# Five loads and stores in another order on SyncE's queue, in an attention and mixture-of-experts kernel

## The chip, the cores and the metric

The kernel runs on one core of one Trainium2 chip. The metric is the device time of one execution in microseconds (us), here the median of three runs. Engines are named as in the profile: PE (TensorE matmuls), PEld (its weight loads), DVE (VectorE), ACT (ScalarE), POOL (GpSimd) and SP (SyncE). SP does no arithmetic; it issues the plain DMA transfers, one after the other.

## The reference

The kernel computes an attention layer whose output goes through a mixture of experts. Cut to its core:

```
scores = q @ k^T / 8; kept: the first 4 keys and the last 128 up to the row's own
a = softmax(scores);  x = a @ v                  # q, k, v: 4 batches, 8 heads, 768 rows, 64 wide
x = x with a row's heads side by side            # 3072 rows of 512
logits = x @ w_gate + log1p(exp(x @ w_noise)) * noise      # 8 experts
top2 = the two best experts of each row, weights by softmax over the two
out[row] = sum over its two experts e of weight * (relu(x[row] @ w1[e]) @ w2[e])   # 512 -> 1024 -> 512
```

## The kernel before

There are two phases. Phase one, about the first 150 us, is the attention, the routing of rows to experts and the preparation of the first expert. Phase two is the experts' matmuls.

In phase one the work is cut into 16 groups, numbered 0 to 15: a batch and a pair of heads each. Every group has three units of 256 query rows, so there are units 0 to 47. A group needs two loads: its keys and queries (`load_kq`, L387, tile `kq`, three buffers) and its values (`load_v`, L390, tile `vn`, two buffers). Of a unit, PE computes the scores (L413), ACT and DVE mask and exponentiate them, PE turns the result (L502), and PE multiplies by the values (L528) and by differences of neighbouring blocks of values (L531). Those differences, tile `dv`, are made on POOL from `vn` by the helper at L320.

Results of a batch leave in two ways into one DRAM buffer, `x_rows`. The attention rows are stored by `rows_d` (L562), four DMAs for 256 rows, once DVE has transposed them (L557). When the batch is routed, the experts' weights of each row are stored beside them by `keep` (L887), four DMAs whose runs are 64 bytes long (6x16 floats a partition); they are called the weight rows below, and their source, tile `rt_w`, is finished on POOL at L883. One more DMA (L1499) fills the first 128 rows of `x_rows` with zeros from tile `zt`, for slots of an expert that hold no row.

The rows of the first expert are fetched from `x_rows` by an indirect DMA on POOL (`gather`, L1028, tile `xg`); the first three such gathers come after batch 1 is routed. The program holds the first of them until the list of its rows (`idg`, DVE L980), the attention rows and weight rows of batches 0 and 1 and the zeros have all been written. The rows are then scaled on DVE (L1080, L1082).

The experts' weights come through tile `st` (`w_chunk`, load at L1138, two buffers); ACT makes the high half (L1142) and POOL or DVE the low half (L320).

The order of all these steps in phase one is a table of numbers, `ORDER`, replayed by `Plan.replay`; every engine executes its own steps in that order. A load takes two numbers, the issue on SP and the transfer; the second emits nothing. A second table, `GATES`, holds some loads back: `803:31` keeps the load of values with number 803 behind the scores of unit 31, `1012:38` the keys of group 15 behind those of unit 38, and `856:42` the next load of values behind those of unit 42. SP waits in order, so whatever stands behind a waiting DMA waits too. The order of phase two comes from `Plan.run`, a planner with costs.

Of the kernel before, what the change touches and what calls it, by code (L numbers as in the profile page):

```python
# [80 lines left out]
"""  # L81
SIDE = """
00000101100011100111100110100100100010101001000001100110100000110001100101100000010010000010010001100000010110010000
# [1540 lines left out]
```

## Time and profile before

| | |
|---|---|
| median of 3 runs | 718.93 us (717.76 to 720.94) |
| the profiled execution | 717.77 us, of which the span of instructions is 716.1 us |
| PE busy | 703.1 us, 98% of the span |
| DVE, ACT, POOL busy | 420.1, 308.1, 386.0 us |
| DMA rate over the span | 145 GB/s |

A share over the whole span mixes the two phases. In phase two PE is the only engine that is always busy. In the stretch that the change touches, about 97 to 118 us, PE, DVE and ACT are all busy nearly all the time, and so are the DMA engines. Whether a transfer that lands earlier or later changes anything is read from the rows of that stretch: who waits for it, and how long before its use it has landed.

### The profile page before, as it was taken

Reading aid. Unit: us, or ns where it says so; the run is one execution under the profiler, and the core shown is the slowest. Engines: PE = TensorE matmul, PEld = TensorE weight load, DVE = VectorE, ACT = ScalarE, POOL = GpSimd, SP = SyncE. Lnnn points to the kernel's source line nnn. Section 1 sums busy time; section 2 is a strip of 40 time slices with the busy share of each in tenths; the row PEclk is TensorE's granted clock in tenths of the full one; section 3 lists DMA queues with packets and bytes.
Section 4 is the critical chain, followed back from the end, with each engine's and each line's share of the span. In section 5 each row is a group of like instructions: output and inputs, shape, how many; then the busy total and the mean of one; then the engine's idle time right before and its main releaser. Section 6 shows DMA issues by size and latency. Waiting matters only on the chain.

```text
span 716.1 us, 16960 instructions
## 1 busy us (share of the span) xinstructions
PE 703.1 (98%) x6580; PEld 626.3 (87%) x6580; DVE 420.1 (59%) x1008; ACT 308.1 (43%) x823; POOL 386.0 (54%) x602
## 2 busy tenths in 40 slices
PE   8999999999999999999999999999999999999996
PEld 4878787768899989989999999999999999999994
DVE  7889999988547545553564366436544734473310
ACT  6999999942244233313331343134313421442210
POOL 3647668711466755465556645663567373737012
PEclk9999999999999999999999999999999999999999
DMA  7566777777866616372737364736554560634023
GB/s 231 194 231 193 184 217 225 167 225 204 293 116 196 169 35 166 129 189 52 178 129 174 62 170 145 167 64 177 178 109 92 165 151 26 155 119 78 6 40 45
DMA packets 68467, 104.63 MB, mean 146 GB/s; under 512 B 20112, under 2 KB 41360, under 8 KB 68384
## 3 DMA queue, kind: packets, MB, share of 16 engines
q1 hardware_dynamic: 55104, 75.71, 34.3%
q0 software_dynamic: 13280, 27.81, 20.5%
q8 instruction: 52, 0.85, 0.5%
q14 instruction: 31, 0.25, 0.1%
HBM read 72.79 MB, written 30.70 MB: 145 GB/s over the span
## 4 chain that ended last, share of the span: by engine, by line
PE 86%; DVE 4%; issue 4%; POOL 2%; DMA 2%; ACT 1%; POOLq 0%; DVEq 0%; ACTq 0%
PE H L1182 12%; PE H L1184 12%; PE H L1183 12%; PE Y L1242 8%; PE Y L1241 8%; PE Y L1240 8%; PE Y L1250 4%; PE Y L1251 4%; PE Y L1249 4%; PE D L413 4%; PE D L502 3%; PE X L528 2%; PE X L531 2%; PE X L543 1%; POOL out L1283 1%
## 5 line engine op out<-in xcount | busy, mean ns | idle before, releaser
L1034 POOL DMA_INDIRECT xg<-x_rows,rt_idq x173 | 174.5, 1009 | 62.8 <-issue 46.1
L1182 PE MATMUL H<-skn,w 128*128 128x384 f32 (+4 forms) x508 | 174.0, 343 | 0.0
L1184 PE MATMUL H<-skn,w 128*128 128x384 f32 (+4 forms) x508 | 173.7, 342 | 0.0
L1183 PE MATMUL H<-sqn,w 128*128 128x384 f32 (+4 forms) x508 | 173.2, 341 | 0.0
L1226 ACT ACTIVATE h<-H 128x384 fp32r<-128x384 f32 (+4 forms) x127 | 63.4, 499 | 250.5 <-PE H L1184 244.8
L1231 DVE SCALAR_TENSOR_TENSOR h<-H,h 128x384 fp32r<-128x384 f32 (+4 forms) x127 | 71.5, 563 | 159.8 <-ACT h L1226 159.7
L1283 POOL DMA_INDIRECT out<-y,idx x46 | 80.8, 1756 | 52.2 <-ACT y L1278 41.0
L1183 PEld LDWEIGHTS H<-sqn,w 128*128 128x128 f32 x508 | 95.5, 188 | 5.1 <-DVE sqn L320 0.2
L1182 PEld LDWEIGHTS H<-skn,w 128*128 128x128 f32 x508 | 95.4, 188 | 5.2 <-DVE lt L753 0.3
L1292 POOL COPY spacer<-h 1x1 f32<-1x1 f32 x88 | 25.0, 284 | 133.7 <-ACT h L1226 133.4
L1184 PEld LDWEIGHTS H<-skn,w 128*128 128x128 f32 x508 | 95.3, 188 | 1.8
L457 ACT ACTIVATE cbuf<-cbuf,nb 128x132 f32<-128x132 f32 x192 | 75.1, 402 | 1.8 <-POOL nb L446 0.9
L1104 ACT ACTIVATE skn<-xtn 128x512 fp32r<-128x512 f32 (+2 forms) x46 | 27.6, 605 | 63.8 <-DVE xtn L1095 63.8
L1242 PE MATMUL Y<-w2a,h 128*128 128x512 f32 x136 | 53.9, 396 | 0.0
L1240 PE MATMUL Y<-w2a,h 128*128 128x512 f32 x136 | 53.6, 394 | 0.0
L1241 PE MATMUL Y<-w2a,h 128*128 128x512 f32 x136 | 53.5, 394 | 0.0
L1240 PE MATMUL Y<-w2b,h 128*128 128x512 f32 x136 | 53.5, 393 | 0.0
L1241 PE MATMUL Y<-w2b,h 128*128 128x512 f32 x136 | 53.4, 393 | 0.0
L1242 PE MATMUL Y<-w2b,h 128*128 128x512 f32 x136 | 53.3, 392 | 0.0
L320 DVE TENSOR_TENSOR w<-st,w 128x1024 fp32r<-128x1024 f32 x30 | 36.6, 1222 | 9.1 <-ACT w L1142 9.0
L413 PE MATMUL D<-kq 64*64 64x200 f32 (+3 forms) x832 | 39.4, 319 | 2.1 <-DVE mn L443 2.1
L320 DVE TENSOR_TENSOR sqn<-xtn,skn 128x512 fp32r<-128x512 f32 (+2 forms) x46 | 30.0, 658 | 17.0 <-ACT skn L1104 16.8
(214 smaller groups left out, 1332.3 us busy)
## 6 DMA issues: line engine op xcount, KB each, us to landing
st<-in_w1l SPq DMA_DIRECT2D x32, 512.0 KB
st<-in_w2l SPq DMA_DIRECT2D x32, 512.0 KB
kq<-in_kq SPq DMA_DIRECT2D x15, 816.0 KB
vn<-in_v SPq DMA_DIRECT2D x16, 384.0 KB
x_rows<-xr SPq DMA_DIRECT2D x48, 128.0 KB
out<-zt SPq DMA_DIRECT2D x24, 256.0 KB
y<-y_rows SPq DMA_DIRECT2D x14, 256.0 KB
xg<-x_rows,rt_idq POOLq DMA_INDIRECT x173, 2.8
```

Of the source, the lines that this page charges most:

```text
L320: eng.tensor_tensor(out, a, b, op=OP.subtract)
L413: last = nc.tensor.matmul(x[:, o:o + w], kq(g)[r, 1, j, t], k[:, f:f + w], start=True, stop=True)
L457: nc.scalar.activation(C(n)[:, u], C(n)[:, u], AF.Exp, bias=get("nb", n)[:, u:u + 1], scale=1.0 / math.sqrt(D), accum_out=get("sm", n // 2 ...
L1034: nc.gpsimd.indirect_dma_start(out=x[:, i, :], out_offset=None, in_=xbuf.rearrange("r (q d) -> (r q) d", d=sh.SW), in_offset=bass.Indirect ...
L1182: nc.tensor.matmul(p, w[:, 0], xh, start=(i == 0), stop=False)
L1183: nc.tensor.matmul(p, w[:, 0], xl, start=False, stop=False)
L1184: nc.tensor.matmul(p, w[:, 1], xh, start=False, stop=(i == sh.DM // 128 - 1))
L1231: nc.vector.scalar_tensor_tensor(h[:, width:2 * width], p, 0.0, h[:, :width].bitcast(F32), op0=OP.max, op1=OP.subtract)
L1240: nc.tensor.matmul(p, hh, w[:, 0], start=(f == 0), stop=False)
L1241: nc.tensor.matmul(p, hh, w[:, 1], start=False, stop=False)
L1242: nc.tensor.matmul(p, hl, w[:, 0], start=False, stop=(f == FC - 1))
L1283: d = nc.gpsimd.indirect_dma_start(out=out, out_offset=bass.IndirectOffsetOnAxis(ap=x[:size(e, t), t:t + 1], axis=0), in_=get("y", Y[e, t] ...
```

## The change

The numbers of five steps stand at other places in `ORDER`. 1132 is the load of the first quarter of `w2` of the first expert. 803 is the load of the values of group 12. 948 and 1012 are the loads of the keys of groups 14 and 15. The weight rows of batch 1 (696) and the zeros (1116) keep their own places and change sides with the loads that move. No instruction is added or removed, and no engine's work but SP's is in another order.

```
@@ ORDER, two of its lines @@
-646 693 734 809 676 666 679 699 700 820 701 698 704 702 648 643 793 810 718 754 692 821 382 694 680 420 755 735 811 513
+1133 686 646 693 734 809 676 666 679 699 700 820 701 698 704 702 648 643 793 810 718 754 692 821 382 694 680 420 755 735
-607 814 1131 756 860 803 804 741 846 766 696 697 742 705 757 707 683 815 743 708 861 758 767 796 862 893 710 746 744 769
+814 1131 756 860 741 846 766 696 697 803 804 948 949 1012 1013 742 705 757 707 683 815 743 708 861 758 767 796 862 893
```

On SP, from the stores of batch 1's attention rows to the values of group 13, this stood before (`x4`: four DMAs in a row):

```order
L562 DMA x_rows<-xr 32x8x128 x8
L1138 DMA st<-in_w2l 128x1024
L390 DMA vn<-in_v 128x768
L887 DMA x_rows<-rt_w 128x6x16 x4
L1499 DMA x_rows<-zt 128x576
L387 DMA kq<-in_kq 128x1632 x2
L390 DMA vn<-in_v 128x768
L379 DMA vr<-in_vs 16x1024 x2
```

The load of weights stood behind both stores of attention rows, the weight rows behind the values of group 12, and both loads of keys behind the zeros. On SP this stands there now:

```order
L562 DMA x_rows<-xr 32x8x128 x4
L1138 DMA st<-in_w2l 128x1024
L562 DMA x_rows<-xr 32x8x128 x4
L887 DMA x_rows<-rt_w 128x6x16 x4
L390 DMA vn<-in_v 128x768
L387 DMA kq<-in_kq 128x1632 x2
L1499 DMA x_rows<-zt 128x576
L390 DMA vn<-in_v 128x768
L379 DMA vr<-in_vs 16x1024 x2
```

The load of weights has moved ahead of the second store of attention rows, the weight rows ahead of the values of group 12, and the keys of groups 14 and 15 to right behind those values; the zeros come last of these.

On POOL the same instructions stand in the same order; only the semaphores that they wait for have other numbers. From the differences for group 12 to the first gather, with the waits as they are now:

```order
L320 TENSOR_TENSOR dv<-vn 128x640 [waits DMAHW7_49,PE_49]
L470 TENSOR_SCALAR sm<-sm 128x8 [waits Activation_49]
L446 TENSOR_SCALAR nb<-mn 128x4 [waits Pool_49]
L1028 DMA xg<-x_rows,idg 128x576 [waits DMAHW3_49,DMAHW4_49,DMAHW2_49,DMAHW5_49,DMAHW1_49,DMAHW6_49,DMAHW0_49,DVE_49]
L446 TENSOR_SCALAR nb<-mn 128x4 [waits Pool_49]
L518 AFFINE_SELECT CM<-CT 128x256 [waits Activation_49]
```

The names `DMAHW0` to `DMAHW7` are eight semaphores that SP's DMAs use in turn. The differences still wait for the load of their values, and the gather for its writes and for DVE's list; what is behind the gather on POOL is what was behind it before.

## Rows read from the trace of the kernel before

**Rows 1.** The page's first part: busy time, share of the span, instructions of each engine.

```profile
PE 703.1 (98%) x6580; PEld 626.3 (87%) x6580; DVE 420.1 (59%) x1008; ACT 308.1 (43%) x823; POOL 386.0 (54%) x602
```

**Rows 2.** PE's waits, 95 to 150 us: who, for what, us, times, longest.

```profile
PE D L1090 <- DVE xg L1082: 0.6, 1, 0.6
...
PE X L528 <- DVE xtn L418: 0.3, 1, 0.3
```

**Rows 3.** Windows: length; PE, PEld, DVE, ACT, POOL busy; clock; DMA share, GB/s.

```profile
100.00:103.00 3.00, 3.00 (x104) 2.58 (x104) 2.81 (x12) 2.98 (x14) 2.57 (x12) 1.00 0.70 175
103.00:109.00 6.00, 6.00 (x176) 4.99 (x168) 5.79 (x17) 5.85 (x26) 3.77 (x5) 1.00 0.92 234
109.00:112.00 3.00, 3.00 (x64) 2.09 (x57) 3.00 (x7) 3.00 (x10) 2.01 (x5) 1.00 0.86 161
112.00:115.00 3.00, 3.00 (x72) 2.02 (x66) 3.00 (x9) 2.84 (x13) 3.00 (x6) 1.00 0.95 349
115.00:118.00 3.00, 2.89 (x86) 2.08 (x86) 2.72 (x9) 3.00 (x15) 2.56 (x6) 1.00 0.53 201
135.00:150.00 15.00, 13.10 (x325) 10.64 (x324) 13.36 (x33) 10.56 (x41) 9.02 (x17) 1.00 0.60 142
```

**Rows 4.** Timeline of SP: start, us until the last is issued, line, transfer.

```profile
97.97 2.23 SPq L562 DMA_DIRECT2D x_rows<-xr  x4
...
101.38 2.25 SPq L562 DMA_DIRECT2D x_rows<-xr  x4
103.73 0.41 SPq L1138 DMA_DIRECT2D st<-in_w2l  x1
105.98 0.36 SPq L390 DMA_DIRECT2D vn<-in_v  x1
106.43 3.27 SPq L887 DMA_DIRECT2D x_rows<-rt_w  x4
109.75 0.53 SPq L1499 DMA_DIRECT2D x_rows<-zt  x1
110.33 2.61 SPq L387 DMA_DIRECT2D kq<-in_kq  x2
117.78 0.33 SPq L390 DMA_DIRECT2D vn<-in_v  x1
...
134.52 0.42 SPq L390 DMA_DIRECT2D vn<-in_v  x1
```

**Rows 5.** Timeline of POOL; in brackets the idle time before and its releaser.

```profile
102.35 0.22 POOL L883 COPY rt_w<-rt_w 128x48 f32<-128x48 f32 x1
...
113.88 1.54 POOL L320 TENSOR_TENSOR dv<-vn 128x640 f32<-128x640 f32 x1
...
116.28 1.23 POOL L1028 DMA_INDIRECT xg<-x_rows,idg  x1 [0.23 <-issue]
...
117.75 1.00 POOL L518 TENSOR_SCALAR_AFFINE_SELECT CM<-CT 128x256 f32<-128x256 f32 x2
...
138.57 1.55 POOL L320 TENSOR_TENSOR dv<-vn 128x640 f32<-128x640 f32 x1
```

**Rows 6.** Timeline of DVE: transposes, list of the gather, first use of gathered rows.

```profile
100.59 0.76 DVE L557 STREAM_TRANSPOSE xr<-xtn 128x256 f32<-128x256 f32 x2
...
115.83 0.15 DVE L980 SCALAR_TENSOR_TENSOR idg<-D,ga 128x3 int32<-128x3 f32 x1
...
120.17 0.22 DVE L1080 TENSOR_SCALAR xg<-xg 128x16 f32<-128x16 f32 x1
```

**Rows 7.** Timeline of PE: scores (L413) and multiplications by the values.

```profile
105.25 0.66 PE L528 MATMUL X<-CT,vn 128*64 128x128 f32 x8
...
116.89 1.49 PE L413 MATMUL D<-kq 64*64 64x132 f32 x36
...
119.16 0.39 PE L531 MATMUL X<-CM,dv 128*64 128x128 f32 x4
```

**Rows 8.** Timeline of ACT: the high half of the moved load of weights.

```profile
109.61 1.05 ACT L1142 ACTIVATE w2a<-st 128x1024 fp32r<-128x1024 f32 x1
```

30 rows, old and new, of the table ORDER are left out of this document.

## The prediction

> **What bounds the kernel now.** I read the busy shares first: PE works 703.1 of 716.1 us, so at most 13.0 us of the span are not matmul time [rows 1]. Next the waits of PE in the stretch that holds the moved transfers and what follows up to the end of phase one: there are four, 1.9 us in all, the longest 0.6 us, and every one ends with DVE, ACT or POOL, none with a DMA [rows 2]. The windows say where: from 100 to 115 us PE is never idle, from 115 to 118 us it is idle for 0.11 us, and the rest of the idle time, 15.00 - 13.10 = 1.90 us, lies behind 135 us [rows 3]. DVE and ACT are nearly full in the same windows (5.79 and 5.85 of 6 us from 103 to 109), and the DMA engines are busy to 0.86 to 0.95 between 103 and 115 us. So three engines and the DMA are all close to full, but what PE waits for is computed data. A transfer that lands earlier can gain only where somebody waits for it; one that lands later costs only once its reserve is used up.
>
> **The change, transfer by transfer.** Nothing is added or removed, so the only terms are times of issue. I go along SP's queue.
>
> The load of weights now follows the first of the two stores, whose issue ends at 97.97 + 2.23 = 100.20. SP then stands idle before the second one, since its transposes run to 100.59 + 0.76 = 101.35 and its first DMA is issued at 101.38 [rows 4, 6]. An issue of 0.41 us fits into that pause: the load goes out near 100.3 instead of 103.73, some 3.4 us earlier, and the store still starts at 101.38 and ends at 103.63. The user of the load is ACT at 109.61, which comes in its order behind other work, with no idle time in brackets before it [rows 8]. Value 0.
>
> The weight rows come next. POOL has them ready at 102.35 + 0.22 = 102.57, before SP is free, so they are not held: they start at 103.7 instead of 106.43, 2.7 us earlier, and end by 103.7 + 3.27 = 107.0 [rows 4, 5]. Only the first gather needs them. It also needs DVE's list, which is ready at 115.83 + 0.15 = 115.98, and it starts 0.30 us after that [rows 5, 6]. DVE sets it, so the gain is 0.
>
> The values of group 12 fall back. Before they were issued at 105.98, right behind the multiplication that frees their buffer (105.25 + 0.66 = 105.91) [rows 4, 7]. Now they go out at about 107.0, 1.0 us later. How long such a load takes is bounded by the last group's: issued at 134.52, used by POOL at 138.57, so it lands within 4.05 us [rows 4, 5]. That gives 111.1 at the latest here, and POOL takes them at 113.88: 2.8 us of reserve. Value 0.
>
> The keys of groups 14 and 15 go out at about 107.4 to 110.0 instead of 110.33 to 112.94. Their gate, the scores of unit 38, stands on PE ahead of the multiplication that starts at 105.25, so it holds nothing [rows 7]. PE uses the first of them at 116.89, with no idle time in brackets, so landing sooner gains 0 [rows 7].
>
> The zeros change from 109.75 to about 110.0 at the issue, 0.25 us, but two loads of keys are now ahead of them. This is the one edit that can cost, because the first gather waits for the zeros too. I take the DMA engines' work from the windows: 0.70x3 + 0.92x6 + 0.86x3 + 0.95x3 + 0.53x3 = 14.64 us between 100 and 118 [rows 3]. The changed kernel has the load of weights ready in the slack of the first window, so that I let the engines run at 0.92 throughout: 14.64 / 0.92 = 15.9, and the last of it, the zeros among it, is through at 115.9. That is just as the list is ready (115.98). The bounds are 114.6 (engines full from 100 on) and 118.0 (nothing won). At 114.6 the gather is not held at all; at 118.0 it is held for 2.0 us. Value 0, by the middle case.
>
> From 117.78 on SP's queue is as before: the next load of values is held there by unit 42's scores, which started at 116.89 [rows 4, 7]. So nothing of the new order is carried past this point by SP.
>
> The sum is 0.0 us against the profiled execution's own 717.77 us. That execution stands 1.16 us below the median of the three runs, 718.93; I forecast for the median 718.8 us.
>
> **A rule that speaks against the new order.** The window with most of the weight rows moves 161 GB/s at a DMA share of 0.86, the next one, with the keys, 349 GB/s at 0.95 [rows 3]. The Trainium skill, "DMA: Bandwidth & Descriptors", Specifications, gives 512 bytes as the least transfer for full rate; these runs have 64 bytes. The trace agrees that the engines are occupied with few bytes there. By that rule the weight rows, put ahead, would push the values back by their whole stretch.
>
> **The rivals.** *Slower, by the zeros.* The DMA engines take what SP issues in turn, so the zeros land with the last of the keys, later than 116.4. The Trainium skill, "DMA: Bandwidth & Descriptors", Queues, rings and completion order, says that each DMA engine takes the descriptors of one queue in ring order; no row here shows which packet went first. The gather stands on POOL ahead of the selections (117.75) that PE needs at 119.16 [rows 5, 7]. The first is done by half of 1.00 us, 118.25, the second by 118.75, so PE has 0.4 us of reserve; a gather held for 2.0 us costs 2.0 - 0.4 = 1.6 us. For it speaks that POOL has no way around a held gather; against it the estimate of 115.9. Time: 718.93 + 1.6 = 720.5.
>
> *Slower, by the weight rows.* If they hold the DMA engines for as long as one window, 3.0 us, the values land at 111.1 + 3.0 = 114.1 and POOL is held for 0.2 us at 113.88; against it stands the 4.05 us, which is an upper bound. Time: at most 719.1.
>
> *Faster.* The keys are through before the gathers' rows are fetched, so the gathers find free DMA engines, and DVE's chain runs ahead. For it: the DMA share is 0.53 from 115 to 118 us and could be lower. Against it: DVE takes the first gathered rows at 120.17 with no idle time in brackets, so it did not wait for them [rows 6]. The most that can be won is the idle time of PE behind 135 us, 1.9 us, if all of it went: 717.0.
>
> *The change does nothing*, since the weight rows are not ready and hold the values: POOL's 102.57 against 103.7 on SP speaks against it, and the time would be that of before or of the second rival.
>
> **How the numbers follow.** No change: 0.70, with 717.3 to 720.0 as its own range (the sum at the profiled execution and at the median, with the runs' scatter around it). Slower by the zeros: 0.17, 718.9 to 720.5. Faster: 0.10, 717.0 to 718.9. The weight rows or no effect: 0.03. A measurement of this kernel can tell about 0.5% from no change, 3.6 us. No case reaches this bound: the dearest is 1.6 us and the best gain 1.9 us. What is left for over 3.6 us is a median that drifts, since the three runs lie 3.2 us apart, together with a wait behind 118 us that the rows of before can't show: 0.04 faster, 0.03 slower, 0.93 within. The range has to hold the two outer cases and part of that scatter: 716.6 to 720.9.
>
> **What would show it.** In the profile of the changed kernel SP should issue the load of weights at about 100.3, the weight rows from 103.7, the values near 107.0, the keys near 107.4 and the zeros near 110. The differences on POOL should start near 113.9 and the first gather near 116.3. PE's scores near 116.9 should have no idle time before them, and PE's idle time from 95 to 150 us should stay near 2 us. The first rival shows as idle time of POOL before the gather that ends with a DMA, and a wait of PE behind it for the selections. I am wrong on the whole if the idle time of PE in this stretch changes by more than 2 us, or if phase two, whose order is untouched, takes another time.

## The result and the profile after

The changed kernel takes 722.78 us (median of 11 runs, 720.80 to 725.91) against 719.55 us for the kernel before beside it on the same chip (11 runs, 717.72 to 721.06). The ratio is 1.0052 [1.0033, 1.0070]: slower by half a per cent, 3.2 us. The forecast was 718.8 us and no change that can be measured, with 0.03 for slower. It was wrong. The likeliest way to be slower had been named, the zeros that land behind the keys, but its price was set at half of what it is.

The profiled execution of the changed kernel took 723.43 us, its span is 721.8 us. The page's first part shows that the matmul time is nearly what it was [rows 1]; PE's idle time went from 13.0 to 17.3 us.

```profile
PE 704.5 (98%) x6580; PEld 626.5 (87%) x6580; DVE 420.9 (58%) x1008; ACT 308.7 (43%) x823; POOL 386.2 (54%) x602
```

The windows say where. First the kernel before from 95 to 127 us (length; busy time of PE, PEld, DVE, ACT, POOL; clock; DMA share and GB/s):

```profile
95.00:127.00 32.00, 31.84 (x817) 24.66 (x809) 30.71 (x98) 30.69 (x123) 25.11 (x54) 1.00 0.79 220
```

The same view of the changed kernel:

```profile
95.00:127.00 32.00, 28.57 (x713) 21.59 (x706) 26.91 (x82) 27.31 (x109) 22.34 (x48) 1.00 0.70 196
...
150.00:225.00 75.00, 74.18 (x477) 62.68 (x474) 48.33 (x135) 25.66 (x44) 27.84 (x43) 1.00 0.72 212
225.00:235.00 10.00, 8.63 (x55) 7.88 (x55) 7.11 (x18) 3.32 (x5) 6.88 (x9) 1.00 0.52 178
```

PE is busy 3.27 us less in the stretch of the moved transfers. The other visible gap, 1.4 us from 225 to 235 us, lies in phase two, whose order is untouched; from 150 to 240 us PE is idle for 2.19 us here, but also for 1.71 and 2.11 us in two of the kernels below that take the time of before (weight rows alone, zeros early), so I count it as scatter. The same windows in steps of 3 us, of the changed kernel:

```profile
103.00:106.00 3.00, 3.00 (x64) 2.42 (x66) 2.99 (x9) 3.00 (x13) 2.24 (x3) 1.00 0.94 252
106.00:109.00 3.00, 3.00 (x104) 2.61 (x107) 2.80 (x8) 2.83 (x13) 1.33 (x4) 1.00 0.56 61
109.00:112.00 3.00, 3.00 (x52) 2.00 (x44) 3.00 (x7) 3.00 (x10) 2.23 (x7) 1.00 0.91 294
112.00:115.00 3.00, 2.89 (x67) 1.94 (x64) 3.00 (x8) 2.83 (x13) 3.00 (x5) 1.00 0.96 348
115.00:118.00 3.00, 2.17 (x50) 1.03 (x50) 2.14 (x8) 2.01 (x10) 0.56 (x3) 1.00 0.39 150
118.00:121.00 3.00, 2.45 (x48) 1.74 (x46) 2.14 (x7) 2.54 (x11) 1.43 (x3) 1.00 0.38 97
```

From 115 us on all four compute engines have idle time, POOL by far the most (0.56 of 3.00 us against 2.56 before, [rows 3]). Before that the DMA engines run at 0.56 of their time and 61 GB/s from 106 to 109 us, where the kernel before has a share of 0.92 over 103 to 109 us [rows 3]: the DMA work did not come forward as the forecast assumed. SP's timeline shows why (columns as in [rows 4]):

```profile
100.00 0.41 SPq L1138 DMA_DIRECT2D st<-in_w2l  x1
101.04 2.71 SPq L562 DMA_DIRECT2D x_rows<-xr  x4
103.85 3.98 SPq L887 DMA_DIRECT2D x_rows<-rt_w  x4
107.93 0.49 SPq L390 DMA_DIRECT2D vn<-in_v  x1
108.46 0.91 SPq L387 DMA_DIRECT2D kq<-in_kq  x2
109.42 0.43 SPq L1499 DMA_DIRECT2D x_rows<-zt  x1
```

Until 107.93 only weight rows are issued, 3.98 us long and few bytes. Then values, both loads of keys and the zeros go out within 1.9 us. The zeros are issued 0.33 us earlier than before (109.75, [rows 4]), with 2 x 816 KB of keys just ahead.

When the zeros land is seen on POOL's sequencer, whose waits the profile lists under POOLq. Ahead of the first gather it waits for one semaphore after another; the row gives the number of these waits, the shortest, median and longest in ns, and when the first and the last began. The kernel before:

```profile
L1028 POOLq EVENT_SEMAPHORE  x3: 43/43/300, 113.7 to 113.8; - x3
```

The changed kernel:

```profile
L1028 POOLq EVENT_SEMAPHORE  x4: 17/43/5020, 113.3 to 118.5; - x4
```

Before, the longest wait is 0.30 us and the last begins at 113.8, so all the writes have landed by about 114.1. Now one wait lasts 5.02 us, and the last one begins at 118.5. The semaphore events of the trace say what the long wait is for: the semaphore of one store of weight rows, complete at 108.92, and that of the zeros. A DMA from SP adds sixteen completions to its semaphore, and the sixteenth of the zeros comes at 118.38 us, 9.0 us after the issue (before at 114.11, 4.4 us after it). Fifteen of them are in by 116.88; the last one alone is 1.5 us later. POOL then, in the changed kernel:

```profile
113.55 1.54 POOL L320 TENSOR_TENSOR dv<-vn 128x640 f32<-128x640 f32 x1
...
115.50 0.23 POOL L446 TENSOR_SCALAR nb<-mn 128x4 f32<-128x4 f32 x1
119.52 1.23 POOL L1028 DMA_INDIRECT xg<-x_rows,idg  x1 [3.80 <-PE D L413]
120.79 0.24 POOL L446 TENSOR_SCALAR nb<-mn 128x4 f32<-128x4 f32 x1
120.98 1.00 POOL L518 TENSOR_SCALAR_AFFINE_SELECT CM<-CT 128x256 f32<-128x256 f32 x2
```

The differences start at 113.55, no later than before (113.88, [rows 5]), so the values were in time. The gather stands 3.80 us later than POOL could start it; before it was 0.23 us [rows 5]. The name in the bracket, a score of PE, is a coincidence of ends: the instruction order of the changed kernel gives the gather seven waits for DMA and one for DVE, none for PE, and the experiments below show other names there. Between the last of the waits (118.5) and the start of the gather lies 1.0 us. DVE is next. Its list is ready at 115.49 + 0.16 = 115.65, and it has 2.50 us of idle time until the gathered rows land:

```profile
115.49 0.16 DVE L980 SCALAR_TENSOR_TENSOR idg<-D,ga 128x3 int32<-128x3 f32 x1
...
121.11 0.35 DVE L821 SCALAR_TENSOR_TENSOR rt_ab<-lg 128x48 f32<-128x48 f32 x1
123.97 0.28 DVE L1080 TENSOR_SCALAR xg<-xg 128x16 f32<-128x16 f32 x1 [2.50 <-DMA xg<-x_rows,idg]
124.28 0.69 DVE L1082 TENSOR_TENSOR xg<-xg 128x512 f32<-128x512 f32 x1
124.89 0.45 DVE L436 COPY_PREDICATED cbuf<-le,D 128x256 f32<-128x256 uint8 x1
```

Before, the first use of the gathered rows stands at 120.17 without a wait [rows 6]. And PE, its rows with idle time in this stretch:

```profile
117.44 0.63 PE L742 MATMUL D<-xtn,wbd 128*32 128x256 f32 x4 [0.83 <-issue]
118.00 1.49 PE L413 MATMUL D<-kq 64*64 64x132 f32 x36
...
121.45 0.44 PE L531 MATMUL X<-CM,dv 128*64 128x128 f32 x4 [1.00 <-POOL CM L518]
...
125.40 0.81 PE L413 MATMUL D<-kq 64*64 64x132 f32 x20 [1.43 <-DVE cbuf L436]
```

Three gaps, 0.83 + 1.00 + 1.43 = 3.26 us, are nearly all of the 32.00 - 28.57 = 3.43 us that PE is idle in the window; the kernel before has 0.16 us there. Two of them follow from the gather: PE waits for the selections that stand behind it on POOL, and then for a copy (L436) that stands on DVE behind the use of the gathered rows. The first gap, inside one step's matmuls, has no releaser; it comes while the gather is held, but the profile doesn't tie it to the gather. PE's other waits up to 150 us are three of the four of [rows 2]; the fourth now lies behind 150 us.

### The profile page after: what moved, and what is told of

It is laid out like the page before. It is cut to its first block, busy times and chain, and to the rows that moved or that the text cites. A ratio compares the mean times of both kernels' runs of the same rounds, so it can differ in the third digit from the quotient of the medians.

```text
span 721.8 us, 16961 instructions
## 1 busy us (share of the span) xinstructions
PE 704.5 (98%) x6580; PEld 626.5 (87%) x6580; DVE 420.9 (58%) x1008; ACT 308.7 (43%) x823; POOL 386.2 (54%) x602
## 4 chain that ended last, share of the span: by engine, by line
PE 83%; DMA 5%; issue 4%; DVE 3%; POOL 2%; ACT 1%; SPq 0%; POOLq 0%; DVEq 0%; ACTq 0%
PE H L1182 12%; PE H L1184 12%; PE H L1183 12%; PE Y L1242 8%; PE Y L1241 8%; PE Y L1240 8%; PE Y L1249 3%; PE Y L1250 3%; PE Y L1251 3%; PE D L413 3%; PE D L502 3%; PE X L528 2%; PE X L531 2%; DMA kq<-in_kq 2%; PE X L543 1%
## 5 line engine op out<-in xcount | busy, mean ns | idle before, releaser
L413 PE MATMUL D<-kq 64*64 64x200 f32 (+3 forms) x832 | 39.2, 317 | 3.2 <-DVE cbuf L436 1.4
```

## The experiments

The theory: two loads of keys ahead of the zeros delay the landing of the zeros, and the first gather holds POOL, then DVE and PE. The rivals: the small transfers of the weight rows, or the load of weights, now ahead of other transfers, take DMA time where it hurts; or the early keys disturb the stretch as such, whatever the zeros do. Ratios are to the kernel before on the same chip.

**One part at a time.** Three kernels are the kernel before with one part of the change each. In the table the change moves four loads, not five steps (1132, 803, 948 and 1012); the two loads of keys move together here.

```
@@ ORDER of before: e1_weights @@
-515 516 686 646 ... 859 738 1132 1133 844
+515 516 1132 1133 686 646 ... 859 738 844
@@ ORDER of before: e2_weight_rows @@
-756 860 803 804 741 846 766 696 697 742
+756 860 741 846 766 696 697 803 804 742
@@ ORDER of before: e3_keys @@
-1134 824 1116 1117 ... 711 948 949 784 ... 785 1012 1013 1136
+1134 824 948 949 1012 1013 1116 1117 ... 711 784 ... 785 1136
```

> The kernel before with one edit: the load of weights ahead of the second store of attention rows. Theory 1 (the zeros land behind the two loads of keys and hold the first gather on POOL): zeros and keys stay in their old order, so 719.6 us like before, within 1 us; gather near 116.3. Theory 2 (the loads of keys, closer behind each other and earlier, delay PE's instruction fetch): keys stay where they were, also 719.6. Theory 3 (the load of weights crowds the stores and what follows): part or all of the 3.2 us, 721 to 723.

> The kernel before with one edit: the weight rows ahead of the values of group 12. Theory 1 and theory 2: 719.6 us, within 1 us, since zeros and keys keep their order. The rival of the prediction (the weight rows hold the DMA engines and the values come late): the differences on POOL start later than 114.5 and the time is 720.5 or more.

> The kernel before with one edit: both loads of keys ahead of the zeros. Theory 1: the zeros land after the keys, near 118.5, the gather starts near 119.5 and the time is 722 to 724 us, as long as the whole change. Theory 2: the keys are only 0.6 us earlier than before, so PE's fetch is as before, and the time is 719.6 to 720.2.

Measured: the load of weights alone 720.58 us against 721.46, 0.9993 [0.9980, 1.0005]; the weight rows alone 721.28 us, 0.9998 [0.9981, 1.0014]; the keys alone 725.45 us, 1.0052 [1.0033, 1.0071]. The first two parts cost nothing that can be measured; the third by itself has the whole ratio. The rows of the third, POOL's waits and gather:

```profile
L1028 POOLq EVENT_SEMAPHORE  x4: 17/43/7002, 113.6 to 120.8; - x4
```

```profile
121.81 1.23 POOL L1028 DMA_INDIRECT xg<-x_rows,idg  x1 [5.77 <-issue]
```

Here the zeros are issued last of all, at 113.12, have landed by 120.8, and the gather starts 1.0 us later. That is 2.3 us later than I expected, since SP takes 2.55 us to issue the two loads of keys here (0.91 us in the changed kernel). The gather is held longer than in the changed kernel, so that the two ratios are equal is partly chance. PE in the same kernel:

```profile
118.65 0.66 PE L528 MATMUL X<-CT,vn 128*64 128x128 f32 x8
123.75 0.69 PE L531 MATMUL X<-CM,dv 128*64 128x128 f32 x4 [4.44 <-POOL CM L518]
124.23 1.07 PE L528 MATMUL X<-CT,vn 128*64 128x128 f32 x8
```

The wait for the selections, 1.00 us in the changed kernel, is 4.44 us here. The eight multiplications of L528 take 0.66 us ahead of it and 1.07 us behind it: the granted clock falls, as the windows say:

```profile
121.00:124.00 3.00, 0.25 (x2) 0.25 (x4) 0.00 (x0) 0.64 (x3) 2.14 (x4) 0.87 0.16 33
124.00:127.00 3.00, 3.00 (x64) 2.67 (x66) 1.45 (x4) 1.16 (x7) 2.64 (x5) 0.56 0.47 126
```

**The zeros back in front.** If the keys disturb the stretch as such, the changed kernel stays slow when only the zeros move. Two kernels put the zeros ahead of both loads of keys and between them:

```
@@ ORDER of the changed kernel: e4_zeros_before_keys @@
-803 804 948 949 1012 1013 742 ... 824 1116 1117 759
+803 804 1116 1117 948 949 1012 1013 742 ... 824 759
@@ ORDER of the changed kernel: e8_zeros_between @@
-803 804 948 949 1012 1013 742 ... 824 1116 1117 759
+803 804 948 949 1116 1117 1012 1013 742 ... 824 759
```

> The changed kernel with the zeros put ahead of the two loads of keys. Theory 1: the zeros land before 115, the gather starts near 116 and the time is back at 719.6 us, within 1 us. Theory 2: the gather is back, but PE still has an idle gap of about 0.8 us inside the logits' matmuls (L742) near 116.6, and the time is 720.4 to 721.5.

> The changed kernel with the zeros between the two loads of keys. Theory 1 with transfers taken in turn: the zeros land behind one load of keys, 2 to 3 us earlier than in the changed kernel, near 115.5 to 116.5, so that the gather starts within 1 us of the list; ratio 0.999 to 1.002. If the zeros' landing depends on all traffic and not on the place in the queue, the gather stays near 119.5 and the ratio near 1.005.

Measured: ahead of both 720.46 us against 721.46, 0.9981 [0.9966, 0.9996]; between them 720.55 us against 721.34, 1.0004 [0.9984, 1.0024]. The loss is gone in both, with all four moved loads where the change put them, so the rivals fall. PE's gap of 0.83 us inside L742 is in neither profile. SP's issues in the second:

```profile
108.43 0.43 SPq L387 DMA_DIRECT2D kq<-in_kq  x1
108.91 0.43 SPq L1499 DMA_DIRECT2D x_rows<-zt  x1
109.38 0.43 SPq L387 DMA_DIRECT2D kq<-in_kq  x1
```

and its waits on POOL:

```profile
L1028 POOLq EVENT_SEMAPHORE  x4: 17/43/845, 113.8 to 114.8; - x4
```

```profile
116.38 1.23 POOL L1028 DMA_INDIRECT xg<-x_rows,idg  x1 [0.22 <-issue]
```

With one load of keys ahead and one behind, the zeros land at 114.72, 5.8 us after their issue, though the second keys are issued only 0.47 us after them. With none ahead they land at 114.12, 4.1 us after their issue at 110.07; with both ahead, in the changed kernel, 9.0 us after it. So transfers from SP land in the order of issue here, and 816 KB ahead cost about 2 us the first time and 3 us the second. The Trainium skill, "DMA: Bandwidth & Descriptors", Queues, rings and completion order, says that each DMA engine consumes the descriptors of a ring in order. These three landings agree.

**The zeros much earlier.** The zeros need no data of this stretch, and their gate can be an earlier unit. In the changed kernel and in the kernel before they go out far ahead of it:

```
@@ ORDER and GATES: e5_zeros_early (changed), e6_before_zeros_early (before) @@
-728 611 854 855 ... 824 1116 1117 759
+728 611 1116 1117 854 855 ... 824 759
-1116:39
+1116:33
```

> The changed kernel with the zeros put far ahead, behind the weight rows of batch 0 (with their gate set to unit 33 for that). Theory 1 (the zeros behind the keys hold the first gather, and POOL, DVE and PE wait in its wake): the gather is set by DVE's list again, and the ratio to the kernel before is 0.997 to 1.001. Theory 2 (PE's instruction fetch is late behind the closely packed keys): an idle gap of about 0.8 us inside the logits' matmuls (L742) stays, ratio 1.001 to 1.002. If the other moves of the change cost anything by themselves, the ratio stays above 1.002.

> The kernel before with the zeros put far ahead, at the same place as in the run before this one. Theory 1: in the kernel before the zeros have landed at 114.1, ahead of the list at 116.0, so nothing waits for them and the ratio is 0.998 to 1.001. If the zeros also cost the kernel before something by crowding the keys, 0.995 to 0.998.

Measured: 720.92 us, 0.9996 [0.9979, 1.0012], and 720.95 us, 0.9998 [0.9982, 1.0015], both against 721.34. Without the zeros in the queue the early keys neither cost nor gain anything that can be measured, and in the kernel before the zeros are at no disadvantage where they are.

**The gather out of the way.** If POOL's order passes the delay on to PE, the gather can be put behind the selections of the changed kernel; in a second kernel DVE's first use of the gathered rows also moves, behind five steps of DVE's:

```
@@ ORDER of the changed kernel: e9_gather_later @@
-791 865 997 839 ... 954 829 856
+791 865 839 ... 954 829 997 856
@@ ORDER of e9: e10_gather_and_use_later @@
-998 881 898 ... 852 1019 999
+881 898 ... 852 1019 998 999
```

> The changed kernel with the first gather moved on POOL behind the small step and the two selections that stood behind it; SP's order is that of the changed kernel. Theory 1: the gather still starts near 119.5, DVE still waits for the gathered rows, but PE no longer waits for the selections (1.0 us in the changed kernel); ratio 1.002 to 1.005, about 1 us below the changed kernel. If the held POOL queue is the whole cost, the ratio is back at 1.000 to 1.001; if it is only DVE's wait for the rows, it stays at 1.005.

> The changed kernel with the first gather behind the selections on POOL, as in the last run, and in addition the first scaling of gathered rows (L1080, L1082) moved on DVE behind the five steps that stood behind it; SP's order is that of the changed kernel, so the zeros are as late as there. Theory 1, taken further: the price of the late zeros is what stands behind them in POOL's and DVE's queues, and the fall of PE's clock that follows PE's idle time. Then PE's wait for DVE near 123 us (1.4 us in the run before) shrinks to under 0.5 us, the granted clock stays at 1.00, and the ratio is 0.999 to 1.002. If PE's clock falls because of the late transfers themselves, or something else in the change costs time, the ratio stays at 1.004 to 1.006.

Measured: 724.39 us against 721.34, 1.0050 [1.0033, 1.0067], and 726.39 us against 720.80, 1.0071 [1.0047, 1.0094]. Neither gives the loss back; I had expected the first about 1 us below the changed kernel, and its ratio is the same (1.0050 against 1.0052). In the first, PE's wait for the selections is gone, but DVE has 2.56 us of idle time before the first use, and PE waits 1.4 us for DVE; PE's waits from 118 to 132 us:

```profile
PE D L413 <- DVE cbuf L436: 1.4, 1, 1.4
PE D L502 <- issue: 0.4, 1, 0.4
```

That is less waiting than in the changed kernel. Its windows show what took its place:

```profile
121.00:124.00 3.00, 1.16 (x39) 0.91 (x39) 1.29 (x3) 2.35 (x10) 2.57 (x6) 1.00 0.68 191
124.00:127.00 3.00, 2.98 (x31) 2.18 (x32) 2.51 (x6) 0.40 (x2) 2.98 (x5) 0.50 0.34 98
127.00:130.00 3.00, 3.00 (x49) 2.55 (x49) 2.05 (x9) 2.56 (x11) 0.81 (x4) 0.50 0.74 178
130.00:133.00 3.00, 3.00 (x78) 2.14 (x78) 1.85 (x14) 1.94 (x8) 0.32 (x2) 0.87 0.69 177
```

The clock is 0.50, the 1.2 GHz level, for over 6 us, and PE gets 31 and 49 matmuls done in windows where the kernel before, at 1.00, has 71 and 92. Over all runs, 10 of 11 of this kernel have a mean clock of at most 0.994, of the kernel before beside it 2 of 34. So the edit shows that the chain runs through POOL's order, but the clock takes back what the shorter wait gave, and the time says little on the price of the wait. In the second, DVE:

```profile
124.25 0.23 DVE L1080 TENSOR_SCALAR xg<-xg 128x16 f32<-128x16 f32 x1
124.51 2.73 DVE L1082 TENSOR_TENSOR xg<-xg 128x512 f32<-128x512 f32 x1
```

The multiplication that takes 0.69 us elsewhere takes 2.73 us here, and PE, whose next matmuls need it, stands for 3.25 us. All 12 runs have a mean clock of 0.993 to 0.996. My expectation failed: I had taken the wait away and counted neither on the long instruction nor on the clock.

**The two versions again**, on one chip with one set of runs of the kernel before: the changed kernel with the zeros ahead of the keys, and the changed kernel as it is.

> The run with the zeros ahead of both keys once more, since its ratio was 0.9981 with an interval that ends below 1. If the rest of the change (the earlier load of weights, the weight rows ahead of the values) gains something by itself, the ratio is again 0.997 to 0.999; if that was scatter, 0.999 to 1.001.

> The changed kernel itself once more, beside the two runs above on the same chip. All theories: a ratio of 1.003 to 1.007. Theory 1 with the clock: the runs whose mean granted clock is at or under 0.994 are the longer ones, by 2 to 3 us.

Measured: 720.14 us against 720.80, 0.9982 [0.9962, 1.0003], and 723.44 us, 1.0028 [1.0003, 1.0053], just under the range that I expected. The better version stands at 0.998 both times, once clear of 1 and once not. That it beats the kernel before is not shown: with the same four loads moved and the zeros between the keys or far ahead, the ratios are 1.0004 and 0.9996. Against the changed kernel it is 720.14 / 723.44 = 0.995. The second profile of the changed kernel repeats the chain, with the zeros issued 1.75 us later:

```profile
L1028 POOLq EVENT_SEMAPHORE  x4: 17/43/4642, 115.0 to 119.8; - x4
```

```profile
120.80 1.23 POOL L1028 DMA_INDIRECT xg<-x_rows,idg  x1 [3.41 <-DVE lt L753]
```

```profile
PE X L531 <- POOL CM L518: 2.1, 1, 2.1
...
PE D L413 <- DVE cbuf L436: 0.4, 1, 0.4
```

Again 1.0 us lies between the last wait and the gather; the bracket names another releaser. PE waits 2.1 us for the selections and 0.4 us for DVE, and the gap of 0.83 us inside L742 isn't there. In the three executions whose mean clock is 0.995 or less, the time is 724.37, 725.75 and 727.76 us, above the median in each. In the first set of runs of the changed kernel the three at 0.992 to 0.994 took 725.91, 725.74 and 722.01 us, the last below the median: part of the runs' spread is the clock's, and not all of it.

## Why the prediction was wrong

- The times of issue held to about 1 us. Forecast and measured: load of weights 100.3 and 100.00, weight rows 103.7 and 103.85, values 107.0 and 107.93, keys 107.4 and 108.46, zeros 110.0 and 109.42, differences on POOL 113.9 and 113.55. The weight rows took 3.98 us where I put 3.27, which made values and keys 1 us later than forecast.
- The terms of the load of weights, the weight rows and the values, each put at 0, held: 0.9993 and 0.9998 by themselves, and the differences of POOL were not held. The keys gained nothing by landing sooner, as forecast (0.9996 with the zeros out of the queue).
- **The step that failed is the term of the zeros, "Value 0, by the middle case".** I spread the whole DMA work evenly at a share of 0.92 from 100 us on and so had the zeros land at 115.9. They landed at 118.4, 0.4 us past the upper bound of 118.0. Two things were missing. The sum holds only if there is work issued to fill the engines; in fact they ran at 0.56 from 106 to 109 us, while SP issued weight rows and nothing large until 107.93. What was lost there is by my estimate (0.92 - 0.56) x 3 / 0.92 = 1.2 us, which puts the zeros at 117.1; fifteen of their sixteen completions were in by 116.88. And a landing is the last completion, here 1.5 us behind the others, which a mean share of sixteen engines can't show. The trace of before has it too: 112.71 for fifteen, 114.11 for the last.
- The rival "slower, by the zeros" had the right mechanism and place; it needed a chance well above 0.17. The trace of before already held the fact that should have given it: the keys were issued at 110.33 and the engines were still full to 115 us [rows 3, 4]; whatever is queued behind that lands late.
- Its price, 1.6 us, was also too small, by three terms. The landing was 0.4 us later than the bound. The gather starts 1.0 us after the last wait for the DMAs (118.5 to 119.52, 120.8 to 121.81, 119.8 to 120.80), which the trace of before could not show, since there the writes are in at 114.1 and what comes last is later. That this is DVE's list, as the prediction says, the rows don't tell: the list is ready at 115.98, POOL's own step ahead of the gather ends at 116.06, and the gather follows them by 0.30 and 0.22 us. And I ended the chain at the selections, though DVE's first use of the gathered rows stands ahead of a copy that PE needs: 1.43 us more. The gather started 119.52 - 116.28 = 3.24 us later than before; PE's idle time in the stretch grew by 3.27 us and the median by 3.23 us. The close agreement is partly luck: profiles of kernels that take the time of before have 0.5 to 1.4 us of idle time in this stretch, the one of before 0.16. From 95 to 150 us PE's idle time went from 2.11 to 4.78 us, past the 2 us that the prediction named as the sign of being wrong.
- The range's upper end, 720.9, was built on that price; the chance of 0.03 for slower by 0.5% was built on the same 1.6 us and fell with it.
- Open: what the 0.83 us gap in one profile is, why DVE's multiplication took 2.73 us in the last edit, and whether the zeros ahead of the keys are worth 0.2%.

## What to carry to other kernels

A transfer that is moved ahead in a queue pushes back the landing of what it passes (here 816 KB by about 2 to 3 us); look for the small store that somebody waits for, and put it ahead of the large loads that nobody needs yet. A DMA's landing is reckoned from what was issued ahead of it and when, not from an average share of the engines, and with room for a last part that comes late. When an engine can be held in its order, price the chain through all engines behind it, and keep room in the range for the clock that an idle PE may lose.

## What the runs showed of the hardware

- A store of 288 KB landed 9.0 us after its issue with two loads of 816 KB just ahead, 5.8 us after it with one (108.91 to 114.72) and 4.1 us with none (110.07 to 114.12). The second load, issued 0.47 us behind it, did not hold it back.
- The last of such a store's sixteen completions came 1.5 us behind the fifteenth in the changed kernel and 1.4 us in the kernel before, but 0.04 and 0.03 us with one load of keys ahead and with none. In the changed kernel a packet of 16 KB of the instruction queue ran from 115.03 for 0.96 us; that such a packet holds back one part is not shown.
- POOL started the indirect DMA 0.9 to 1.0 us after the last of its waits for earlier DMAs in all five profiles in which POOL had nothing else to do by then (the two with the later gather: 118.0 to 118.93 and 118.2 to 119.20).
- PE's granted clock fell to the 1.2 GHz level after idle time: 0.25 of 3.00 us busy, then 0.56 (a mean over both levels); 1.16 of 3.00 us busy, then 0.50 for 6 us. In the changed kernel itself PE was busy 2.17, 2.45, 2.52 and 1.60 of 3.00 us in the windows from 115 to 127 us, and the clock stayed at 1.00 in that profile; in its second profile it stayed at 1.00 with 1.27 of 3.00 us busy.
- One DVE multiplication of 128x512 took 2.73 us against a median of 0.69 us. POOL ran its differences (128x640) beside it from 125.17 to 126.69 us. Of the 637 such multiplications in the thirteen profiles it is the only one beside these differences and the only one above 0.76 us; that POOL slows DVE there was not tried.
